# A new global order of the same operations for random-feature attention followed by a low-rank mixer

## The chip, the cores and the metric

One core of one Trainium2 chip. The metric is device time in microseconds (us) of one execution. Engines: PE is TensorE, PEld its weight loads, DVE is VectorE, ACT is ScalarE, POOL is GpSimd, SP is SyncE.

## The reference

```python
# attention with random features: batch 8, heads 8, seq 576, head_dim 64, 128 features
proj = einsum('bhsd,md->bhsm', x, omega)              # for q and for k
phi  = concatenate([cos(proj), sin(proj)]) / sqrt(m)
kv   = einsum('bhsm,bhsd->bhmd', phi(k), v)
z    = sum(phi(k), axis=2)
num  = einsum('bhsm,bhmd->bhsd', phi(q), kv)
den  = einsum('bhsm,bhm->bhs', phi(q), z)             # kept away from 0
x    = (num / den), heads side by side                # (8, 576, 512)
# mixer: U is 576x32, V 32x576, w_ch1 512x2048, w_ch2 2048x512
u    = x + (x^T @ U @ V)^T
out  = u + relu(u @ w_ch1) @ w_ch2
```

## The kernel before

The kernel is a list of named operations, each bound to one engine, and a string of some 1,150 names that says in which order they are issued. An engine takes its own in that order (POOL in before: the load of q2 starts at 11.01 us, behind a quarter turn that had waited 4.47 us for ACT). `tpp` is a PE transpose, `tp` the copy of its result, `ak`/`aq` the projections of k and q, `uk`/`uq` their turning into angles (DVE), `s`, `sk`, `sq` sines (ACT), `p`, `pk`, `pq` the quarter turn that makes cosines of sines (POOL), `c`, `ck`, `cq` sines again, `kv` the product with v (PE), `kvb` its cast (ACT for the first four groups), `num` and `x` the quotient, `hu0`, `ut0` the low-rank step, `w1`, `r`, `w2`, `o` the dense layers. The number behind is the group of two heads (0 to 31), or the pair of groups for loads and transposes. `lowc` is the cast of the low-rank factors U and V (POOL). `@n` names a PSUM bank; `d/n` are dummy matmuls, whose results nobody reads. In the profile lines `raw` is a loaded block of q or k, `T` its transpose, `ang` the angles, `ft` their sines and cosines, `vq` the cast v, and `ps` a PSUM bank; `hid` is a buffer that holds first blocks and low-rank factors before it holds the hidden layer.

```python
def run(self, order):
    for word in order.split():
        ...
        assert name not in issued and all(n in issued for n in needs), word
        if takes:
            self.banks[name] = range(int(at), int(at) + takes)
        ...
        emit()
...
# loads of k, q, v (pair 0) and of the weights are issued by POOL, in program order
add(("ld", name, n), POOL, lambda ...: nc.gpsimd.dma_start(load(name, n), quad(src, n)), needs=need)
nc.gpsimd.dma_start(W1b[:, a, :, :], moe_w_ch1[...])
(nc.sync if n else nc.gpsimd).dma_start(held["v", n], quad(v, n))
...
# the low-rank factors come by SP, and POOL casts them: "lowc"
def cast_low_rank():
    nc.gpsimd.tensor_copy(Ub, U_f)
    V9 = Vf.rearrange("r (p s) -> r s p", s=NS)
    nc.gpsimd.tensor_copy(Vb[:, 0:S].rearrange("r (s p) -> r s p", p=TL), V9)
    nc.gpsimd.tensor_copy(Vb[:, S:S + TL], V9[:, 8, :])
add("lowc", POOL, cast_low_rank, needs=["low"])
...
# POOL also makes the cosine's angle and widens v for the kv product
def quarter(a, g=g):
    nc.gpsimd.tensor_scalar(out=ang, in0=ang, scalar1=TURN / 4.0, scalar2=1.0, op0=ALU.add, op1=ALU.mult)
def widen(n=n):
    nc.gpsimd.tensor_copy(vq[n % NV][:, :, 0:D], held.pop(("v", n)).rearrange(...))
...
add(("hu0", p), PE, ..., needs=[("x", p), "lowc"], takes=1)     # first user of the low-rank factors
```

## Time and profile before

| | before |
|---|---|
| median of 6 runs (range) | 359.53 us (358.76 to 360.26) |
| profiled span | 357.5 us |
| group 0 to 3: quotient `x` starts at | 18.89, 28.77, 32.85, 34.05 us |
| first and last output addition (L653) start at | 66.23 and 353.89 us |

The chain of waits of the kernel before, by engine, and its longest piece outside PE (start, duration, what):

```profile
PE 91%; DMA 4%; issue 1%; DVE 1%; ACT 1%; POOL 1%; POOLq 0%; DVEq 0%
...
11.74 11.71 DMA raw<-in_k_dram
```

Then POOL's time order from 11 to 26 us (start, duration, instruction; in brackets the idle time before it and what ended it):

```profile
11.74 0.72 POOL L302 DMA_DIRECT2D raw<-in_k_dram  x1
...
19.24 0.41 POOL L251 CAST Ub<-hid 128x288 bf16<-128x288 f32 x1
...
21.02 2.10 POOL L424 TENSOR_SCALAR ang<-ang 128x2304 int32<-128x2304 int32 x1
...
25.10 1.15 POOL L309 CAST vq<-vraw 128x1152 bf16<-128x1152 f32 x1
```

To see: POOL issues the fourth k block, for which PE waits later, at 11.74 us (the third q block 0.7 us sooner). From 19.24 us on it runs the three low-rank casts (L251 to L254, 1.8 us) before the quarter turn of group 2 (21.02) and before the second cast of v (25.10). Neither looks like a problem here, because PE waits for the loads until 23.49 us anyway, and ACT behind it from 22.58 to 26.20 us.

### The profile page before, as it was taken

To read this page: it belongs to the slowest core of one execution; us is meant where nothing else is said; L and a number is where in the kernel's file an instruction comes from. 1 tells how busy PE (TensorE), PEld (TensorE's weight loads), DVE (VectorE), ACT (ScalarE), POOL (GpSimd) and SP (SyncE) were. 2 spreads that over 40 slices of the span, in tenths; PEclk is the share of its full clock that TensorE was granted. 3 is DMA by queue.
4 is the path that set the end of the run, shared out by engine and by line. 5 is a ranking of instruction groups with operands and counts; after the bars stand their busy time and mean duration, and the time that the engine had idled before them with its cause. 6 is when DMAs were issued, how large, how long until landed. Compare 5 with 4: busy or idle time off the path is not lost.

```text
span 357.5 us, 8225 instructions
## 1 busy us (share of the span) xinstructions
PE 343.4 (96%) x3551; PEld 181.3 (51%) x3585; DVE 191.7 (54%) x277; ACT 218.3 (61%) x230; POOL 117.3 (33%) x100
## 2 busy tenths in 40 slices
PE   7859999999999999999999999999999999999997
PEld 3547455455555645455465445454445544444444
DVE  3959667795598558348697437365422440100121
ACT  4858899649859887767746586823686405535100
POOL 5796645528155607226432205500520000000000
PEclk9978999999999999999999999999999999999999
DMA  8998799999969997861973416735421060320224
GB/s 208 214 211 169 130 176 206 207 140 281 164 82 202 238 204 123 140 205 23 232 140 66 97 35 187 126 68 102 113 54 38 0 100 19 70 64 0 59 61 88
DMA packets 68567, 45.06 MB, mean 126 GB/s; under 512 B 47156, under 2 KB 59828, under 8 KB 68532
## 3 DMA queue, kind: packets, MB, share of 16 engines
q1 hardware_dynamic: 55348, 30.09, 39.3%
q0 software_dynamic: 12816, 13.93, 23.8%
q8 instruction: 28, 0.46, 0.5%
q10 hardware_dynamic: 368, 0.52, 0.4%
q14 instruction: 7, 0.06, 0.1%
HBM read 37.16 MB, written 9.44 MB: 130 GB/s over the span
## 4 chain that ended last, share of the span: by engine, by line
PE 91%; DMA 4%; issue 1%; DVE 1%; ACT 1%; POOL 1%; POOLq 0%; DVEq 0%
PE ps L617 35%; PE ps L637 35%; PE ps L434 5%; PE ps L449 4%; DMA raw<-in_k_dram 3%; PE ps L385 2%; PE ps L411 2%; PE ps L583 2%; DMA hid<-in_k_dram 1%; PE ps L454 1%; PE ps L519 1%; PE ps L325 1%; DVE ang L363 1%; PE ps L591 0%; PE ps L378 0%
## 5 line engine op out<-in xcount | busy, mean ns | idle before, releaser
L420 ACT ACTIVATE ft<-ang 128x2304 bf16<-128x2304 int16 (+2 forms) x67 | 133.7, 2021 | 32.5 <-DVE ang L363 12.0
L637 PE MATMUL ps<-W2b,hid 128*128 128x512 bf16 (+1 forms) x564 | 130.2, 373 | 2.8 <-issue 1.9
L630 ACT ACTIVATE hid<-ps 128x512 bf16<-128x512 f32 x144 | 82.0, 599 | 76.7 <-PE ps L617 76.0
L617 PE MATMUL ps<-uT,W1b 128*128 128x512 bf16 x512 | 118.3, 379 | 0.1
L424 POOL TENSOR_SCALAR ang<-ang 128x2304 int32<-128x2304 int32 (+2 forms) x34 | 68.0, 2000 | 124.8 <-ACT ft L420 106.6
L363 DVE TENSOR_SCALAR ang<-ps 128x1280 int32<-128x1280 f32 (+2 forms) x66 | 85.6, 1315 | 28.5 <-PE ps L379 18.0
L617 PEld LDWEIGHTS <-W1b 128*128 128x128 bf16 x576 | 54.5, 98 | 64.9 <-issue 2.3
L637 PEld LDWEIGHTS <-hid 128*128 128x128 bf16 x592 | 55.3, 98 | 61.7 <-issue 2.1
L653 DVE TENSOR_TENSOR o<-ps,u 128x512 f32<-128x512 f32 x32 | 21.9, 686 | 42.9 <-PE ps L637 40.3
L438 DVE CAST kvb<-ps 128x260 bf16<-128x260 f32 x28 | 11.7, 424 | 31.2 <-PE ps L434 30.3
L465 DVE TENSOR_TENSOR x<-ps,rec 128x640 bf16<-128x640 f32 x32 | 26.4, 825 | 1.1
L434 PEld LDWEIGHTS <-ft 64*128 64x128 bf16 x1152 | 22.3, 95 | 7.6 <-issue 5.7
L585 DVE TENSOR_TENSOR u<-ps,x 128x1024 bf16<-128x1024 f32 x16 | 19.2, 1222 | 12.9 <-PE ps L583 10.9
L434 PE MATMUL ps<-vq,ft 64*128 64x65 bf16 x1152 | 24.7, 193 | 1.5 <-POOL vq L309 1.0
L309 POOL CAST vq<-vraw 128x1152 bf16<-128x1152 f32 x16 | 18.3, 1158 | 21.8 <-DMA vraw<-in_v_dram 21.6
L449 PEld LDWEIGHTS <-ft 128*128 128x128 bf16 x512 | 19.9, 99 | 5.7 <-issue 1.0
L449 PE MATMUL ps<-kvb,ft 128*128 128x65 bf16 x512 | 21.8, 195 | 0.0
L617 PE MATMUL ps<-utailT,W1b 128*128 128x512 bf16 x64 | 15.0, 379 | 0.0
L385 PE MATMUL ps<-WT,T 64*128 64x128 bf16 x256 | 13.4, 228 | 0.5 <-DVE ang L363 0.4
L411 PE MATMUL ps<-T,WT 64*128 64x512 bf16 x64 | 13.5, 401 | 0.1
L385 PEld LDWEIGHTS <-T 64*128 64x128 bf16 x256 | 8.7, 99 | 7.7 <-issue 7.0
L593 DVE TENSOR_TENSOR utail<-ps,x 64x512 bf16<-64x512 f32 x8 | 5.5, 685 | 12.9 <-PE ps L591 12.5
(64 smaller groups left out, 158.4 us busy)
## 6 DMA issues: line engine op xcount, KB each, us to landing
out_dram<-o SPq DMA_DIRECT2D x70, 128.0 KB, 2.5
vraw<-in_v_dram SPq DMA_DIRECT2D x15, 576.0 KB, 5.6
raw<-in_k_dram POOLq DMA_DIRECT2D x14, 288.0 KB, 7.8
raw<-in_q_dram POOLq DMA_DIRECT2D x14, 288.0 KB, 8.9
W1b<-in_moe_w_ch_dram POOLq DMA_DIRECT2D x4, 512.0 KB, 7.0
W2b<-in_moe_w_ch_dram POOLq DMA_DIRECT2D x4, 512.0 KB, 11.9
vraw<-in_v_dram POOLq DMA_DIRECT2D x1, 576.0 KB, 6.2
ang<-in_q_dram ACTq DMA_DIRECT2D x1, 288.0 KB, 3.5
```

The lines of the kernel that those rows point to most:

```text
L363: nc.vector.tensor_scalar(out=dst, in0=src, scalar1=TO_UNITS, scalar2=None, op0=ALU.mult)
L385: nc.tensor.matmul(pk[:, e, i * P:(i + 1) * P], kT[r, c, :], WT[r, :])
L411: nc.tensor.matmul(pq[:, e, :], WT[r, :], transposed("q", n)[r, c:c + 4, :])
L420: nc.scalar.activation(out=held["ft", g].rearrange("p f a c -> p f (a c)")[:, f, lo:hi], in_=low[:, lo:hi, 0], func=ACT.Sin, scale=TO_RAD)
L424: nc.gpsimd.tensor_scalar(out=ang, in0=ang, scalar1=TURN / 4.0, scalar2=1.0, op0=ALU.add, op1=ALU.mult)
L434: nc.tensor.matmul(kv_ps[:, hh, o], ft[r, f, 0, c:c + M], vq[n % NV][r, NS * (g % 2) + s, :], start=(s == 0), stop=(s == NS - 1))
L449: nc.tensor.matmul(nd[:, hh, t, :], ft[:, f, 1, c:c + P], kvb[:, hh, f, :], start=(f == 0), stop=(f == 1))
L465: nc.vector.tensor_tensor(out=x[:, :, hp * P:(hp + 1) * P].rearrange("p t (h d) -> p h t d", h=2), in0=nd[:, :, :, 0:D], in1=rec.unsqueeze ...
L617: nc.tensor.matmul(one(key), W1b[:, f // 4, ct, f % 4 * P:(f % 4 + 1) * P], uT[:, :, ct, :], start=(ct == 0), stop=(ct == NCT - 1))
L630: nc.scalar.activation(out=held["hid", b][:, f, :], in_=one(at_bank), func=ACT.Relu)
L637: nc.tensor.matmul(one(key)[:, 0:cs.stop - cs.start], held["hid", b][:, f, t * P:(t + 1) * P], W2b[:, f, cs], start=(f == 0), stop=(f == N ...
L653: nc.vector.tensor_tensor(out=held["o", b, t][:, cs], in0=one(key)[:, 0:cs.stop - cs.start], in1=u[:, t, cs], op=ALU.add)
```

## The change

The intent is an order found by a search under three assumptions on how the hardware and the software DMA queues share the engines while the kernel opens. Only the order string and the bank numbers in it change; the rest of the program is equal. The whole string differs, so the diff is cut to the opening:

```diff
 ORDER = """
-begin first/k/0 first/k/1 ident first/q/0 om ld/k/0 d/0@4 warm ld/q/0 d/1@4 d/2@5 ld/k/1 d/3@1 d/4@2 ldv/0 d/5@7 ld/q/1 cast/k/1 cast/k/0
-omb ld/k/2 omt@4 tpp/k/0/0@7 tpp/k/0/1@2 tpp/k/0/2@1 tp/k/0/0 WT cast/q/0 tp/k/0/1 akh/0/0@2 tp/k/0/2 akh/0/1@5 tpp/q/0/0@4 ukh/0/0
 ... (cut)
-ld/q/2 tpp/q/1@6 ck/0 ld/k/3 tp/k/1 aq/1@3 pq/0 tp/q/1 d/8@1 uq/1 ak/2@0 wv/0 cq/0 aq/2@6 uk/2 s/1 ld/q/3 ldv/2 kv/0/0@4 W1/0 kv/0/1 uq/2
-ak/3@1 d/9@0 kvb/0 p/1 d/10@0 uk/3 d/11@7 s/2 num/0 d/12@0 tpp/k/2@6 x/0 lowc c/1 tp/k/2 tpp/q/2@4 tpp/k/3@2 p/2 tp/q/2 aq/3@0 kv/1/0@6
 ... (cut)
+begin first/k/0 first/k/1 ident first/q/0 om ld/k/0 d/0@7 warm d/1@1 ld/q/0 d/2@0 ld/k/1 d/3@5 d/4@0 ld/q/1 d/5@7 d/6@4 ldv/0 cast/k/1
+cast/k/0 d/7@0 omb ld/k/2 d/8@5 d/9@6 ld/q/2 omt@5 tpp/k/0/0@0 tpp/k/0/1@2 d/10@3 WT cast/q/0 tp/k/0/0 tp/k/0/1 ld/k/3 gate tpp/k/0/2@0
+low d/11@2 akh/0/0@4 tp/k/0/2 W1/0 tpp/q/0/0@2 ukh/0/0 d/12@7 tpp/q/0/1@1 tp/q/0/0 ld/q/3 akh/0/1@6 tp/q/0/1 aq/0@2 ukh/0/1 W1/1 d/13@5
 ... (cut)
+kv/3/0@2 kvb/2 kv/3/1 ld/k/4 cq/3 uq/4 num/2 lowc kvb/3 x/2 num/3 s/4 ld/q/4 hu0/0@4 x/3 hu0/1@1 W1/3 hu0/2@5 aq/5@6 huc0/0 ut0x/0@0 p/4
 ... (cut; about 1,000 more names in another order up to the end)
```

## The prediction

> **What bounds the kernel now.** I read the summary and the 40 slices first. PE is busy 343.4 of 357.5 us, from the third slice on at 90% or more. The unprofiled median is 359.88 us, about 2.4 us above the profiled span, and I carry that difference over.
>
> ```profile
> span 357.5 us, 8225 instructions
> PE 343.4 (96%) x3551; PEld 181.3 (51%) x3585; DVE 191.7 (54%) x277; ACT 218.3 (61%) x230; POOL 117.3 (33%) x100
> PE   7859999999999999999999999999999999999997
> PEclk9978999999999999999999999999999999999999
> ```
>
> To see: only the first four or five slices (some 9 us each) are not full, and the clock dips in slices 3 and 4. Next, busy time by stretches that I cut where something changes.
>
> ```profile
> 14.00:18.00 4.00, 2.61 (x69) 1.98 (x70) 4.00 (x4) 4.00 (x4) 3.12 (x4) 1.00 1.14 217
> 18.00:23.00 5.00, 1.58 (x25) 1.11 (x21) 3.07 (x6) 4.58 (x3) 5.00 (x5) 0.94 1.16 262
> 23.00:29.00 6.00, 5.51 (x86) 4.17 (x88) 3.91 (x6) 2.80 (x3) 3.22 (x4) 0.50 1.01 186
> 40.00:354.00 314.00, 310.89 (x3092) 160.70 (x3124) 162.32 (x231) 190.55 (x199) 89.59 (x66) 1.00 0.60 117
> ```
>
> The columns are PE, PEld, DVE, ACT, POOL busy, then clock, DMA share, GB/s. To see: from 40 to 354 us PE is busy 310.9 of 314, so an order can win little there unless it removes PE work. From 18 to 23 us PE is nearly idle while DMA is full. From 23 to 29 us it runs at half clock. Then the waits and the time order of PE and ACT there.
>
> ```profile
> PE ps L325 <- DMA raw<-in_k_dram: 2.0, 1, 2.0
> PE ps L325 <- DMA raw<-in_q_dram: 1.9, 1, 1.9
> ACT kvb L438 <- PE ps L434: 3.6, 1, 3.6
> ...
> 20.85 0.68 PE L325 MATMUL ps<-ident,raw 128*128 128x128 bf16 x9 [1.94 <-DMA raw<-in_q_dram]
> 23.49 1.14 PE L325 MATMUL ps<-ident,raw 128*128 128x128 bf16 x9 [1.97 <-DMA raw<-in_k_dram]
> 26.20 0.38 ACT L438 CAST kvb<-ps 128x260 bf16<-128x260 f32 x1 [3.62 <-PE ps L434]
> ```
>
> To see: two PE transposes wait for the q2 and k3 loads (third q block, fourth k block); the kv products of group 1 stand behind them in program order, and ACT, otherwise occupied from 13.8 us, stands 3.62 us for them. The chain of waits says the same: 11.71 us of it, 11.74 to 23.44, is the DMA raw<-in_k_dram. Last, the queues:
>
> ```profile
> q1 hardware_dynamic: 323, 0.61, 88.2%
> q0 software_dynamic: 8, 0.01, 1.6%
> ...
> q0 software_dynamic: 1022, 1.09, 80.7%
> q1 hardware_dynamic: 450, 0.86, 35.2%
> ```
>
> The first pair is 12 to 15 us, the second 15 to 23. q2 was issued at 11.01, behind a POOL wait for ACT of 4.47 us, when the software queue had run dry; the hardware queue (low-rank factors and the second v load) then had the engines. q2 landed after 9.8 us, k3 after 11.7.
>
> [...] The 35.2% beside 80.7% is such sharing; the 88.2% beside 1.6% is not: with a late arrival one queue had everything. So a fair-share model is not safe, which fits a search under three assumptions. [...] In the trace, all k, q and weight loads are POOL issues, so POOL's program order is their order. [...]
>
> **The change part by part.** No arithmetic is added or removed; all 20 dummy matmuls remain, as do all loads. The order of every engine changes from its first items to its last.
>
> Loads. Before, POOL issues k0 q0 k1 v0 q1 k2, then the quarter-turn addition of group 0, then q2, k3, and after two more computations q3 and W1/0. After, it issues k0 q0 k1 q1 v0 k2 q2 k3 W1/0 q3 W1/1 in a row. At about 0.72 us each the eighth ends near 7.2 us, so q2 and k3 are queued 4 to 5 us earlier, and the queue cannot run dry. Alone, the software queue finished v0, q1, k2 at 9.6, 11.0, 12.4 (issue plus landing time), thus 1.4 us per 288 KB. After: q1 9.7, v0 11, then k2, q2, k3 at 12.4, 13.8, 15.2 if undisturbed. The hardware queue must also fit V, U, v1 (1.0 MB, about 4 us at the 0.25 MB/us of those stretches) and v2 (0.58 MB, 2.4 us). If it all goes first, k3 lands at about 15.2 + 6.4 = 21.6. An estimate: 15 to 21.6, against 23.44.
>
> First products. Ten dummies now stand before the omega transpose instead of six. From 1.36 us at 0.43 us each they end at 5.6, and the transpose had been at 4.80: 0.8 us later, of which some comes back since k0, which PE needs at once, lands only at 5.77, and the clock should warm earlier (before, 128-column transposes still took 1.94/18 = 0.108 us at 10.6 to 12.5, and faster ones followed). I book +0.2.
>
> ACT, the engine that paces 13 to 32 us. Rows: 2304-wide sine 2.12, 1280-wide 1.26, 1024-wide 1.05, kvb cast 0.36. DVE must give uq/1 before ACT starts group 1. With tp/k/1, uk/1, tp/q/1, uq/1 (0.75, 1.49, 0.75, 1.22) interleaved with PE from 10.7, I get 15.7 against 14.9 before: +0.8 including the +0.2. From there without a gap: s/1 17.8, kvb 18.1, s/2 20.2, c/1 22.3, sk/3 23.45, c/2 25.6, kvb/1 25.9, sq/3 26.95, ck/3 28.2, kvb/2 28.55, cq/3 29.6, kvb/3 29.95. Before, kvb/3 ended at 32.19. Sum: -3.6 (the wait gone) +0.8 and +0.6 for pieces that come earlier in the new order = -2.2 us. The kv products of group 1 need k3 transposed: PE reaches them near 23 even with k3 at 21.6, 2 us before ACT asks.
>
> DVE alongside: uk/3, tp/k/2, x/0, tp/q/2, uq/3, tp/k/3, uk/4, uk/5, x/1, uq/4, x/2, x/3 at their mean times put x/3 at 32.5, before 34.87. Then uq/5, a hu cast, the first uT piece: 34.75, against 36.24 before. PE enters the dense W1 stretch at about 34.8 with ak/0-5, aq/0-5 and all ut0 products done. Before, at 35.35, it had yet to do aq/5, one ut0x and three ut0 products (0.32 + 0.22 + 0.64 = 1.2 us) and lost another 0.35 on waits up to 37.98. So 0.55 + 1.2 + 0.35 = 2.1 us. A dummy before 46.8 us no longer stands in the dense part: 0.2. Gain in the opening 2.3 us.
>
> The rest, 40 to 354 us. 3.1 us of PE idle is all there is; a new order may win or lose around 1 us of it. I put 0. The end (half tile, last addition, store) is the same. 359.88 - 2.3 = 357.6, rounded to 357.5.
>
> **Rivals.** First: the stall only moves. With hardware traffic at full strength and W1/0 in front of q3, k3 could come after 23 us, or ACT's wait could be replaced by DVE's work, which in my list is full from 15 to 34 us. For: DVE is at 4.00 of 4.00 in 14 to 18. Against: k3 has slack. It would make 359 to 361. Second: the clock. After the early dummies none is left before 46 us; PE has gaps near 13, 17 and 19 us, and before, four dummies stood at 16.5 to 18.4. If it drops to half near 20 us, the products at 22 to 30 cost about 1.5 us more, partly beside ACT: 358.5. If the early dummies keep it warm, DVE starts sooner and 356.5 results. Third: the search has also tightened the middle and PE's cold 6 us vanish wholly from the path: 354 to 355. For: PE was held back by more than ACT at 23 to 29. Against: ACT and DVE sums above set the pace anyway.
>
> **Range and chances.** The opening's gain is 1 to 4 us, the middle +-1.5, runs spread 1.5. So 357.5, range 354.2 to 360.2. Faster by over 2% means under 352.7, and the whole of ACT's wait plus all of PE's idle in the middle would be needed: 0.04. Slower by over 2%, over 367: 0.01. Within: 0.95.
>
> **What would show it.** Right: no wait of PE on raw over 0.5 us between 18 and 24; ACT's 3.6 us before the kvb cast gone; k3 landed by 21.6; kvb/3 done near 30; dense W1 from about 35 instead of 38; the stretch 40 to 354 with PE within 1 us of the same idle. Wrong: ACT gaps of the same sum elsewhere before 35 us, a clock of 0.5 over several us near 20, or PE idle after 40 us above 5 us, for instance behind later W2 loads or wv/2, which now stand behind more on POOL.

The marked cuts are statements of how the hardware behaves that no trace or run of this case shows. None of them is a term of the sum, which stands as it was: 359.88 - 2.3 = 357.6, rounded to 357.5. With "such sharing" read: both queues at work in one stretch, 80.7% and 35.2% from 15 to 23 us.

## The result and the profile after

| | before | after |
|---|---|---|
| median of 6 runs (range) | 359.53 us (358.76 to 360.26) | 357.06 us (356.33 to 357.47) |
| ratio, 95% interval | | 0.9928 (0.9912 to 0.9944) |
| profiled span | 357.5 us | 354.6 us |
| `x` of groups 0 to 3 starts at | 18.89, 28.77, 32.85, 34.05 us | 19.83, 27.04, 29.37, 30.57 us |
| first and last output addition | 66.23, 353.89 us | 61.30, 350.90 us |

A ratio here is the mean time of one kernel's fast runs over that of the other's of the same rounds, so not quite the ratio of the medians. After is 0.7% faster: within 2%.

Summary, slices and chain by engine of the kernel after:

```profile
span 354.6 us, 8256 instructions
PE 345.6 (97%) x3585; PEld 180.4 (51%) x3585; DVE 191.6 (54%) x277; ACT 218.4 (62%) x230; POOL 117.1 (33%) x100
PE   8779999999999999999999999999999999999997
PEclk9789999999999999999999999999999999999999
...
PE 95%; ACT 2%; DVE 1%; POOL 1%; issue 1%; POOLq 0%; DVEq 0%; ACTq 0%
```

To see: no transfer is left on the chain; its 4% of DMA became 2% of ACT and more PE. The dip of the clock came one slice sooner. Beware of one number: PE has 3585 matmul records here and 3551 before. Records are missing in the trace of before, so the 3 us of PE idle that its rows show between 40 and 354 us are mostly not real. From its first to its last output addition before took 287.66 us, and two later kernels with the same tail (e1, e5), whose traces show PE busy 285.00 of 285 us between 65 and 350 us, took the same 287.65 and 287.66 us.

ACT's time order in the kernel after, then where POOL issues the fourth k load and does the low-rank casts:

```profile
13.39 4.23 ACT L420 ACTIVATE ft<-ang 128x1280 bf16<-128x1280 int16 x3 [1.37 <-POOL ang L424]
17.53 0.35 ACT L438 CAST kvb<-ps 128x260 bf16<-128x260 f32 x1
17.78 7.36 ACT L420 ACTIVATE ft<-ang 128x2304 bf16<-128x2304 int16 x4
25.05 0.35 ACT L438 CAST kvb<-ps 128x260 bf16<-128x260 f32 x1
...
28.64 0.37 ACT L438 CAST kvb<-ps 128x260 bf16<-128x260 f32 x1
```

```profile
6.18 0.76 POOL L302 DMA_DIRECT2D raw<-in_k_dram  x1
...
28.90 0.44 POOL L251 CAST Ub<-hid 128x288 bf16<-128x288 f32 x1
```

To see: the idle time of 3.62 us before the second `kvb` cast is gone, ACT runs without a gap from 13.39 to 31.07 us, and the fourth `kvb` starts at 28.64 us instead of 31.82. The k load is issued 5.6 us earlier and lands after 13.9 us, at about 20.1 us instead of 23.44. PE has no wait on a load between 13 and 34 us any more. It starts the first dense product (L617) at 33.73 us, and by 40 us it has started 25 of them, where before had started 11.

All of the gain is made before the first output addition. There after is 4.9 us ahead, of which it gives back 1.9, as its order has left more work for later (289.60 against 287.66 us from first to last addition). Most of the 1.9 us can be counted: 573 second-layer products (L637) come after the first addition in after and 565 in e1 and e5, which have the tail of before, and eight of 0.216 us (in after a row of eight at 61.66 us took 1.89 us, the last of them 0.38) are 1.7 us. At the last addition 3.0 us remain.

### The profile page after: what moved, and what is told of

It reads as the page before. It is cut to its first block, busy times and chain, and to the rows that moved or that the text cites. A ratio compares the mean times of both kernels' runs of the same rounds, so it can differ in the third digit from the quotient of the medians.

```text
span 354.6 us, 8256 instructions
## 1 busy us (share of the span) xinstructions
PE 345.6 (97%) x3585; PEld 180.4 (51%) x3585; DVE 191.6 (54%) x277; ACT 218.4 (62%) x230; POOL 117.1 (33%) x100
## 4 chain that ended last, share of the span: by engine, by line
PE 95%; ACT 2%; DVE 1%; POOL 1%; issue 1%; POOLq 0%; DVEq 0%; ACTq 0%
PE ps L637 36%; PE ps L617 35%; PE ps L434 6%; PE ps L449 5%; PE ps L385 2%; PE ps L411 2%; PE ps L583 2%; PE ps L232 2%; ACT ft L420 2%; PE ps L325 1%; PE ps L454 1%; PE ps L519 1%; DVE ang L363 1%; PE ps L591 0%; PE ps L378 0%
## 5 line engine op out<-in xcount | busy, mean ns | idle before, releaser
L420 ACT ACTIVATE ft<-ang 128x2304 bf16<-128x2304 int16 (+2 forms) x67 | 133.3, 2020 | 29.1 <-DVE ang L363 18.4
L637 PE MATMUL ps<-W2b,hid 128*128 128x512 bf16 (+1 forms) x592 | 135.7, 374 | 0.0
L617 PE MATMUL ps<-uT,W1b 128*128 128x512 bf16 x512 | 119.3, 379 | 0.0
L637 PEld LDWEIGHTS <-hid 128*128 128x128 bf16 x592 | 55.6, 98 | 63.5 <-issue 2.9
L617 PEld LDWEIGHTS <-W1b 128*128 128x128 bf16 x576 | 54.4, 98 | 63.8 <-issue 1.6
L449 PEld LDWEIGHTS <-ft 128*128 128x128 bf16 x512 | 20.1, 99 | 6.7 <-issue 2.1
L438 DVE CAST kvb<-ps 128x260 bf16<-128x260 f32 x28 | 11.7, 424 | 13.6 <-PE ps L434 12.7
L463 DVE RECIPROCAL ps<-ps 128x10 f32<-128x10 f32 x32 | 7.1, 223 | 17.2 <-PE ps L454 17.2
L617 PE MATMUL ps<-utailT,W1b 128*128 128x512 bf16 x64 | 14.8, 379 | 0.0
L302 POOL DMA_DIRECT2D raw<-in_k_dram x14 | 10.1, 725 | 11.1 <-DMA T<-raw 8.0
```

The costliest lines, as they stand in the source:

```text
L420: nc.scalar.activation(out=held["ft", g].rearrange("p f a c -> p f (a c)")[:, f, lo:hi], in_=low[:, lo:hi, 0], func=ACT.Sin, scale=TO_RAD)
L449: nc.tensor.matmul(nd[:, hh, t, :], ft[:, f, 1, c:c + P], kvb[:, hh, f, :], start=(f == 0), stop=(f == 1))
L617: nc.tensor.matmul(one(key), W1b[:, f // 4, ct, f % 4 * P:(f % 4 + 1) * P], uT[:, :, ct, :], start=(ct == 0), stop=(ct == NCT - 1))
L637: nc.tensor.matmul(one(key)[:, 0:cs.stop - cs.start], held["hid", b][:, f, t * P:(t + 1) * P], W2b[:, f, cs], start=(f == 0), stop=(f == N ...
```

## The experiments

Theory at the start: the gain comes from the early loads of q2 and k3, which free ACT. Rivals: it comes from another part of the opening, from the clock, or from the order of the rest. The theory fell in e1; the second theory, that the loads and the low-rank casts on POOL are two waits side by side, was formed on its trace and tested by e5, e10 and e11.

There were twelve runs, of eleven new kernels and of after once more, on three chips (e1 to e4, e5 to e8, e9 to e12), all in five rounds against the kernel before on the same chip. All gave correct results. "Last `x`" is the start of the quotient of group 3.

| run | ratio to before, 95% interval | span, us | last `x`, us | last addition, us |
|---|---|---|---|---|
| e1 before, early loads | 1.0004 (0.9983 to 1.0025) | 356.7 | 33.20 | 353.04 |
| e2 after, late loads | 0.9977 (0.9956 to 0.9999) | 356.8 | 32.83 | 353.17 |
| e3 after's opening, before's rest | 0.9991 (0.9974 to 1.0008) | 356.8 | 31.39 | 353.12 |
| e4 before's opening, after's rest | 1.0057 (1.0031 to 1.0082) | 359.3 | 33.68 | 355.65 |
| e5 before, early loads and late low-rank casts | 0.9944 (0.9918 to 0.9971) | 354.3 | 30.78 | 350.62 |
| e6 after, two copies swapped | 0.9931 (0.9907 to 0.9956) | 354.0 | 30.03 | 350.37 |
| e7 after, nine more dummies | 0.9973 (0.9947 to 0.9999) | 355.8 | 31.73 | 352.15 |
| e8 after, dummies spread | 0.9955 (0.9925 to 0.9984) | 355.1 | 31.08 | 351.52 |
| e9 after again | 0.9955 (0.9927 to 0.9983) | 355.7 | 30.84 | 352.05 |
| e10 before, late low-rank casts | 1.0000 (0.9966 to 1.0034) | 357.6 | 34.10 | 353.93 |
| e11 after, early low-rank casts | 1.0014 (0.9986 to 1.0041) | 357.5 | 33.50 | 353.84 |
| e12 after, swap and late sine | 0.9984 (0.9953 to 1.0015) | 356.3 | 30.81 | 352.61 |

### e1: the early loads alone

```diff
 omb ld/k/2
+ld/q/2 ld/k/3
 ...
 uk/1 sq/0
-ld/q/2
 tpp/q/1 ck/0
-ld/k/3
```

> The kernel before, with only two loads moved: q2 and k3 are issued on POOL right behind k2, ahead of the first quarter-turn addition. Everything else keeps the order of before. Theory (late issue of q2 and k3 makes ACT's 3.6 us wait): the wait before the second kvb cast shrinks from 3.6 to under 1.2 us, PE waits on raw under 0.5 us each, and the time falls by 2 to 3 us, nearly all of the change's 2.5. Rival A (the new compute order in the opening makes the gain): under 1 us of gain, and ACT waits as long elsewhere before 33 us. Rival B (the clock): with PE's gap at 18 to 23 gone, no half-clock stretch at 23 to 29; if that is most of it, the gain comes with ACT's wait still over 1.5 us.

Measured: 1.0004. The theory missed: no gain, although the span is 0.8 us shorter and PE waits for no block of the two loads. PE, ACT and POOL of e1, each from its time order:

```profile
27.98 1.82 PE L434 MATMUL ps<-vq,ft 64*128 64x65 bf16 x72 [2.55 <-POOL vq L309]
```

```profile
22.82 0.35 ACT L438 CAST kvb<-ps 128x260 bf16<-128x260 f32 x1
24.84 4.23 ACT L420 ACTIVATE ft<-ang 128x2304 bf16<-128x2304 int16 x3 [1.66 <-POOL ang L424]
```

```profile
20.88 0.42 POOL L251 CAST Ub<-hid 128x288 bf16<-128x288 f32 x1 [1.50 <-DMA hid<-in_moe_U_dram]
...
22.68 2.12 POOL L424 TENSOR_SCALAR ang<-ang 128x2304 int32<-128x2304 int32 x1
...
26.77 1.15 POOL L309 CAST vq<-vraw 128x1152 bf16<-128x1152 f32 x1
```

To see: the `kvb` cast is on time (22.82 instead of 26.20), but right behind it ACT waits 1.66 us for an angle, and PE waits 2.55 us for the cast of v. Both hang on POOL, which stood 1.50 us for the U factor and worked 1.8 us on the low-rank casts before it came to the quarter turn of group 2. A wait on a load became a wait behind another load, one engine further. This is a reading so far; e5, e10 and e11 test it.

### e2: the late loads alone, in the order of after

```diff
-... ld/q/2 ... ld/k/3 ... W1/0 ... ld/q/3 ... W1/1 ... W1/2      (all before cq/0)
+ut/0 pk/0 ld/q/2 ld/k/3   ...  wv/0 ld/q/3 W1/0   ...  p/2 W1/1   ...  pq/3 W1/2
```

> The kernel after, with its opening loads put back among POOL's computations as before had them (q2 and k3 behind the first addition, q3 and W1/0 behind the first v cast, W1/1 and W1/2 later). Theory: PE waits for raw return, ACT gets a wait of 2 to 4 us before a kvb cast near 23, and the time is 1.5 to 3.5 us over the kernel after, so 356.5 falls back to 358.5 to 360.5. Rival A (compute order): within 1 us of the kernel after, since its order would absorb the lateness.

Measured: 0.9977, so 0.5% or about 1.75 us behind the 0.9928 of after, inside what was expected; but the 0.9928 is from other rounds, and against the 0.9955 of e9 only about 0.8 us are left, with intervals that overlap. ACT's wait before a `kvb` cast was expected at 2 to 4 us near 23 us and was 1.05 us at 25.8 us. PE's transposes of e2 wait again, 1.10 us for the third q block and here for the fourth k block:

```profile
23.97 1.14 PE L325 MATMUL ps<-ident,raw 128*128 128x128 bf16 x9 [1.29 <-DMA raw<-in_k_dram]
```

So the waits on loads come back when the loads are late. That the time needs the early loads in the order of after is suggested, not shown: e2 moved six loads, its clock was at half from 13.7 to 27.4 us (13.4 to 20.3 us in after), and the loss is not clear of e9.

### e3 and e4: openings and rests crossed

```diff
 e3:  the words of after up to w1/0/3, then what is left in the order of before (4 banks chosen anew)
 e4:  the words of before up to w1/0/3, then what is left in the order of after
```

> The first part of the kernel after (up to the fourth first-layer group of batch 0), then the order of the kernel before for all that is left (four PSUM banks reassigned). Theory (all of the gain is made in the opening, the rest is neutral): 2 to 3.5 us faster than before. Rival (the search also tightened the rest): under 1.5 us faster.

> The mirror image: the opening of the kernel before up to the same group, then the order of the kernel after (one PSUM bank reassigned). Theory: within 0.7 us of before. Rival (the rest tightened): over 1 us faster than before.

Measured: e3 0.9991 instead of 2 to 3.5 us gained, e4 1.0057 instead of before's time. Both missed, and the profiles point to the seam, where the two orders meet. Waits of PE of e4 from 34 to 62 us, and PE's share from 40 to 60 us in e3 and then in e4 (PE, PEld, DVE, ACT, POOL busy; clock; DMA share; GB/s):

```profile
PE ps L617 <- ACT hid L630: 1.1, 1, 1.1
PE ps L617 <- DMA W1b<-in_moe_w_ch_dram: 0.3, 1, 0.3
```

```profile
40.00:60.00 20.00, 19.02 (x245) 9.97 (x243) 12.55 (x17) 17.54 (x19) 11.35 (x10) 1.00 1.20 177
```

```profile
40.00:60.00 20.00, 18.57 (x201) 8.99 (x199) 10.90 (x15) 18.26 (x22) 12.88 (x12) 1.00 1.02 165
```

After has 19.99 of 20 us there. So each order's stretch from 34 to 60 us fits its own opening. e3 also had half the clock from 25.5 to 28.9 us (0.72 in the mean of 24 to 30 us), which after had not, and its last `x` 0.8 us later than after. The far tail is neutral: from first to last output addition e3 took 287.65 us, as before; e4 289.61 us, as after.

### e5: early loads and late low-rank casts

```diff
 as e1, and
 tpp/k/2 x/0
-lowc
 ...
 uq/4 pq/3
+lowc
```

> The kernel before with q/2 and k/3 loaded right behind k/2 (as in e1) and, beside that, the low-rank step on GpSimd (the casts of U and V that wait for their load) moved behind pq/3. e1 gave 1.0004 of before. Theory: in e1 that step took the place of the wait on the load of k/3, as GpSimd stood in it for about 3.4 us between p/1 and pk/3 while ScalarE's sines and TensorE's transposes waited for its angles and casts. Then this run is 1.0 to 2.5 us under before (ratio 0.993 to 0.997), k/v bank wait on GpSimd's cast of vq gone, and ScalarE's waits for angles between 10 and 40 us under 2.5 us in sum. Rival: the gain of the opening is lost at its junction with the stretch from 40 to 60 us, as in e3; then this run is within 0.5 us of e1 and of before, even though x of the last group begins 1 us or more sooner than the 33.2 us of e1.

Measured: 0.9944, 1.5 us under before by the medians (356.28 and 357.77 us), and 2.4 us under e1 in span. PE and POOL of e5:

```profile
26.39 0.75 PE L434 MATMUL ps<-vq,ft 64*128 64x65 bf16 x36 [0.71 <-DVE x L465]
```

```profile
20.07 2.10 POOL L424 TENSOR_SCALAR ang<-ang 128x2304 int32<-128x2304 int32 x1 [0.41 <-ACT ft L420]
...
24.47 1.14 POOL L309 CAST vq<-vraw 128x1152 bf16<-128x1152 f32 x1
```

To see: POOL's quarter turn of group 2 starts at 20.07 instead of 22.68 us, the cast of v at 24.47 instead of 26.77, and the wait of 2.55 us for it is gone. ACT's waits for POOL's angles between 10 and 40 us are one of 0.4 us. Nothing of the tail was changed, so the rival (that the gain is lost at the seam) falls for this case. Three names moved (`ld/q/2`, `ld/k/3`, `lowc`) reach 0.9944, between the 0.9928 and the 0.9955 that the whole new order gave: no run shows a gain from the other thousand names.

One rival is left in part, the clock. After its first clock record at 10.17 us the profiled run of e5 has no half clock before the end of the work, while before had it from 22.4 to 29.3 us and e1 from 8.6 to 15.4 and from 29.1 to 32.5 us; part of the 2.4 us of span can be that. The times speak against its being all: of the runs with a mean clock of 0.995 on this chip, e5's three took 355.20, 356.53 and 356.98 us, and before's three 357.11, 357.21 and 358.92 us. After itself gained with 6.8 us of half clock.

### e10: late low-rank casts alone

```diff
 tpp/k/2 x/0
-lowc
 ...
 uq/4 pq/3
+lowc
```

> The kernel before with the low-rank step on GpSimd moved behind pq/3 and nothing else; with before, e1 (early loads alone: 1.0004) and e5 (both: 0.9944) it completes the square. Theory (two waits side by side, the later one counts): the load of k/3 still lands at about 23.4 us and TensorE still waits for it, so 0.9975 to 1.001 of before, no gain from this part alone; the wait of the transposes for raw is there with 2 us or more. Rival (the low-rank step is the cause by itself, and the early loads matter only a little): 0.994 to 0.9965.

Measured: 1.0000. PE and ACT of e10:

```profile
23.54 1.14 PE L325 MATMUL ps<-ident,raw 128*128 128x128 bf16 x9 [1.82 <-DMA raw<-in_k_dram]
```

```profile
26.26 0.38 ACT L438 CAST kvb<-ps 128x260 bf16<-128x260 f32 x1 [3.04 <-PE ps L434]
```

POOL's quarter turn of group 2 starts at 20.07 us here too, but the k load is as late as in before and ACT stands for it. The expectation's "2 us or more" for PE's waits on raw was slightly missed: one wait of 1.82 us. Taken together: loads alone 1.0004, casts alone 1.0000, both 0.9944. The two waits lie side by side, and in the order of before only removing both gave time.

### e11: the casts put back early in the order of after

```diff
 kvb/0 p/1
+lowc
 ...
 uq/4 num/2
-lowc
```

> The kernel after with the low-rank step on GpSimd at the place it has in before, behind p/1, and nothing else. Theory (in e1 that step took the wait's place): the U load lands about 18 to 19 us, GpSimd stands in the step 2.5 to 4 us, ScalarE waits for angles and banks, and the run is 1.0 to 3.0 us slower than e9 (0.996 to 1.001 of before). Rival (the step hurts only next to the rest of before's order): within 0.4 us of e9.

Measured: 1.0014 against 0.9955 of e9 on the same chip, 2.15 us by the medians (358.95 and 356.80). ACT and PE of e11:

```profile
24.30 2.12 ACT L420 ACTIVATE ft<-ang 128x2304 bf16<-128x2304 int16 x1 [1.33 <-POOL ang L424]
```

```profile
26.73 1.04 PE L449 MATMUL ps<-kvb,ft 128*128 128x65 bf16 x16 [3.32 <-ACT kvb L438]
```

POOL stood 2.5 us in the step, the lower end of what was expected: 0.71 us for U and 1.8 us of casts. The quarter turn of group 2 came at 22.15 us (19.99 in after), ACT stood 1.33 us for it, and PE 3.32 us for the `kvb` cast (1.79 in after). The clock was at half from 15.5 to 19.0 and from 25.8 to 32.6 us, and the last `x` came 2.7 us later than in e9. How much of those 2.7 us is the wait and how much the half clock is not separated.

### e6, e7 and e8: ACT's order and the dummies

```diff
 e6
 tp/q/1 W1/2
-cq/0
+ck/0
 ... ak/2 wv/0
-ck/0
+cq/0
```

```diff
 e7 (d: one more dummy)
 sq/0 ak/1
+d
 uk/1 tpp/q/1
+d
 ... (seven more: two behind aq/1, one each behind ak/2 and aq/2, two behind ak/3, one behind tpp/k/2)
```

```diff
 e8
-d/6 ... d/13    (behind ld/q/1 to behind W1/1)
+eight at the places of e7 (one only behind aq/1)
```

> The kernel after with one swap on ScalarE: the copy ck/0 ahead of cq/0, because ScalarE stood still 1.37 us from 12.0 to 13.39 us for the matmul behind which cq/0 waits. Theory (ScalarE sets the pace of the opening from 13 us on): 0.4 to 1.0 us faster than after, so about 0.990 of before, and the first x 0.4 to 0.9 us earlier or the last x 0.4 to 0.9 us earlier. Rival (the pace is set by the matmuls at half clock or by GpSimd's angles): within 0.3 us of after's 0.9928, with a new wait of ScalarE for angles of about the same length.

> The kernel after with nine more dummy matmuls among the TensorE work between 10 and 19 us, to keep the clock from falling to half in 13.7 to 20.3 us. Theory (ScalarE, not TensorE, sets the pace there): even if the clock stays up, within 0.5 us of after (0.9915 to 0.9942 of before). Rival (the half clock costs): 0.8 to 1.5 us faster than after, 0.989 to 0.9905 of before. If the clock falls all the same, the run says only what nine dummies cost: 0.2 to 0.5 us slower.

> The kernel after without its eight early dummies d/6 to d/13, and with eight put between 10 and 19 us in their place. Theory: the early ones run while TensorE waits for its first input anyway, so to take them away gains nothing, and within 0.5 us of after. Rival 1: the early ones warm the clock (full at 6.5 to 6.9 us in after, at 12.4 us in before) and without them the first projections run at half clock and ScalarE's first copy comes later: 0.5 to 1.5 us slower than after (0.994 to 0.997 of before). Rival 2: they hold up the first transposes; 0.5 us faster.

Measured: e6 0.9931, e7 0.9973, e8 0.9955. e6's profile shows the wait of 1.37 us for the angle down to 0.42, and first and last `x` 0.4 to 0.5 us earlier than in after; in time it can't be told from after, whose two sets gave 0.9928 and 0.9955. e7 was expected to change nothing or to gain, or, if the clock fell all the same, to lose 0.2 to 0.5 us. The clock fell, later; the ratio is above those of both sets of after by 0.6 to 1.6 us, though its interval overlaps that of e9. With the extra dummies the clock stayed up until 26.8 us (13.4 us in after), but then it fell. The stretch from 24 to 30 us of e7, then of after:

```profile
24.00:30.00 6.00, 4.30 (x119) 3.87 (x118) 4.21 (x6) 5.98 (x8) 5.12 (x7) 0.74 0.96 163
```

```profile
24.00:30.00 6.00, 4.13 (x142) 3.58 (x142) 5.20 (x9) 5.97 (x8) 5.12 (x7) 1.00 1.09 171
```

To see: the eighth column, the clock, 0.74 against 1.00; PE is as busy, with 119 matmuls done in place of 142. The last `x` is 1.2 us later than in after. In e8 the clock falls at the same time (26.8 us), and the last `x` is 0.5 us later; without the early dummies its first record of full clock is at 13.17 us, against 6.62 us in after. So the profiles read as if half clock while ACT sets the pace (13.4 to 20.3 us in after) cost little, and right before the dense stretch about a microsecond; in e7 part of that is the dummies' own time, which no run separates. e8's time is within the spread of after, so it decides nothing about the dummies in front.

### e9 and e12: after again, and the candidate

> The kernel after, unchanged, on the same chip as e10 to e12, as the measure for them. Every theory expects the earlier ratio again: 0.990 to 0.995 of before, profiled span 354 to 355 us.

e9 gave 0.9955 and a median of 356.80 us; its ratio is 0.0005 and its span (355.7 us) 0.7 us above the range expected: that is the size of what five rounds can tell. Its profiled run also had one PE wait of 0.8 us at 96 us for a transposing transfer, which after had not.

```diff
 e12: as e6, and
 num/3
-s/4
 ... ut0x/0
-p/4
 uq/5 huc0/1
+s/4 p/4
```

> The candidate: after with the swap of e6 (ck/0 ahead of cq/0) and, beside it, the sine of the next group (with the angle op behind it) moved on ScalarE behind the first two copies of hu, which stood ready about 0.8 us before ScalarE took them. Theory: the swap's 0.5 us in the profile come through, and the second move adds 0 to 0.4 us as TensorE was busy 5.81 of 6 us from 30 us on: 0.4 to 1.0 us faster than e9, span 353.4 to 354.2 us. [...]

Measured: 0.9984, no faster than e9 (357.60 against 356.80 us by the medians, with intervals that overlap), so the theory missed. ACT of e12:

```profile
29.92 0.27 ACT L547 CAST hu<-ps 128x128 bf16<-128x128 f32 x1 [1.17 <-PE ps L519]
30.80 0.27 ACT L547 CAST hu<-ps 128x128 bf16<-128x128 f32 x1 [0.62 <-DVE rec L464]
30.97 2.13 ACT L420 ACTIVATE ft<-ang 128x2304 bf16<-128x2304 int16 x1
```

The two copies did not stand ready: ACT waited 1.17 and 0.62 us for them while a sine that could run stood behind. The sine came at 30.97 instead of 28.01 us (e6), and PE had a new wait of 1.0 us for a copy of `hu`. The first dense product started at 35.1 us, against 34.0 in e9 and 33.2 in e6. That the swap of e6 helps is thus not confirmed by a time. No version is shown to beat after; e6 has the shortest span (354.0 us), but on another chip.

## Why the prediction was right or wrong

The time (357.5 predicted, 357.06 measured) and the class were right. Its steps fared unequally. Four small readings were off: PE's row is full from the fourth slice on, not the third; the first blocks of k and q are issued by SP and ACT, not POOL; q2 and k3 were queued 5.5 us earlier instead of 4 to 5; and the 359.88 us were the median of the first three runs (359.53 of all six), 2.4 us above the profiled span because the profiled run itself took 359.3.

- **Loads.** Right in size: k3 landed at about 20.1 us, inside the estimate of 15 to 21.6, and PE waits on no load from 13 to 34 us. In after both queues were busy in one stretch, 71.6% software and 44.7% hardware from 12 to 23 us. In before it was 88.2% hardware and 1.6% software from 12 to 15 us, with a software load issued at 11.01 us. That its late arrival was the reason is the prediction's reading: no view tells whether the software queue had packets ready then.
- **What takes the wait away.** Here a step was missing. The prediction booked 3.6 us of ACT's wait as gone because of the loads. e1 shows that the loads alone give nothing in time (1.0004). What made it true is a move that the prediction never mentions: the low-rank casts, put behind `pq/3` on POOL. e5, e10 and e11 show it from three sides. The first rival, "the stall only moves", named DVE and the load as the new wait; it was POOL, and after's order had dealt with it. In e1 the quarter turn started only at 22.68 us, behind a cast that had waited 1.50 us for U, and at 20.07 us where that cast was moved away (e5).
- **ACT's list.** The order was right, the lengths were too long. From the end of the first `kvb` cast to the end of the fourth the prediction has 18.1 to 29.95, 11.85 us; the profile has 17.88 to 29.01, 11.13 us, and the end came 3.2 us sooner than before's 32.19 where 2.2 was booked. It summed durations, but neighbours overlap: three sines of 2.12 and one of 1.26 us make 7.62, and the row of four takes 7.36, so 0.09 us for each of the three seams.
- **Dense part.** 33.73 against 34.8 us predicted for its start, since DVE's chain and ACT's ran earlier. By 40 us after is 14 dense products ahead; at 0.216 us a piece (the first eight of after took 1.89 us, the last of them 0.38) that is 3.0 us, where 2.1 was booked.
- **The rest.** Booked as 0 with 3.1 us of idle. The idle was mostly missing records. The far tail does not depend on the opening (287.65 to 287.66 us in five kernels with before's rest, 289.60 to 289.72 in eight with after's; e9 is the one exception, with 290.48), and the 1.9 us between the two are mostly the eight products counted above. The stretch from 34 to 60 us is not neutral, as e3 and e4 show; in after it is full (19.99 of 20 us).
- **The clock.** In before the clock was at half from 22.4 to 29.3 us, after PE had been busy 1.58 of the 5 us from 18 to 23, with waits of 1.94 and 1.97 us. In after it fell at about 13.4 us with no idle stretch of PE over 0.42 us between 9 and 13.4 us; PE was busy 0.58 to 0.89 of each microsecond from 9 to 13 us. So what makes the clock fall is not shown: that gaps of PE do it, as the second rival and rival B of e1 have it, was the assumption. The second rival's event came: half clock from 13.4 to 20.3 us in after. Its cost of 1.5 us, an estimate, is not seen: ACT ran without a gap from 13.39 us on. The predicted early warming came too: the same 512-column projection takes 0.39 us for a pair at 8.47 us in after, and 0.61 us at 8.28 us in before, where 0.39 is first seen at 12.46 us. The clock of a profile is no reading before its first clock record: in before the view shows 1.00 from 4 to 22 us, but the first record is at 12.19 us; in after it is at 6.62 us. The stretches of half clock in the opening lasted 6.8 us in before, after, e9, e10 and e12, 3.4 us in e6, e7 and e8, one of each in e1 and e11, and 13.6 us in e2.

In sum: 2.3 us predicted, 2.5 us measured by the medians. That the sum fits is in part luck. The casts, without which e11 lost the whole gain, were not in it, and the sines booked too long made its gain too small. What stays open: the share of the half clock in the losses of e1 and e11 and in the gain of e5, whether after's order needs the early loads (e2), and the choice between after and e6.

## What to carry to other kernels

When a wait is removed, look along the queue of every engine that feeds the one that waited: an instruction that was harmless in the shadow of the old wait (here 1.8 us of casts and their load on GpSimd) can become the next wait, and then the two have to move together. Test the parts in a square (neither, each, both), since one part alone can read as worth nothing (1.0004 and 1.0000 here, 0.9944 together). An instruction put early on the belief that its input is ready holds up those behind it (1.17 and 0.62 us in e12): read first when its input is written.
